# Sums emptied at set later items, and two more passes in 64-row mode, in a fused convolution and two-layer kernel

## The chip, the cores and the metric

The kernel runs on one core of a Trainium2 chip. The metric is device time of one execution in microseconds (us), the median of several runs. The engines are named as in the profile: PE (TensorE, the matmuls), PEld (its weight loads), DVE (VectorE), ACT (ScalarE), POOL (GpSimd) and SP (the queue that issues the DMAs).

## What is computed

A dynamic convolution along the sequence is followed by two fully connected blocks. Cut to what matters:

```python
w = softmax(weight_gen, axis=-1)                 # (2, 4096, 8 heads, 7 taps)
out = einsum('bshk,bskhg->bshg', w, unfolded_x)  # 7 taps back in time, 24 channels a head
x = out.reshape(8192, 192)
h = x @ w_in                                     # 192 -> 2048
g = where(h >= 1, h, where(h <= -1, 0, (h + 1)**2 / 4))
x = g @ w_out                                    # 2048 -> 192: layer 1 ends here
h = x @ w_in2
g = h - tanh(h)
y = g @ w_out2                                   # layer 2
```

Everything is fp32. The kernel keeps that accuracy by splitting each operand into a rounded part (fp32r) and the rest, and multiplying high by high, high by low and low by high.

## The kernel before

The 8192 tokens are cut into 16 blocks of 512. In the code a pass is named by `m` (0 is layer 1, 1 is layer 2) and the block `b`. The 2048 hidden columns of a pass are 16 **items** `f` of 128. An item is: five matmuls into a bank `h` (from `a`, the turned rows of layer 1, or `b`, those of layer 2, and `win`); on ACT and DVE the nonlinearity into `g`; on ACT the high part `gh` (L801); on DVE the low part `gl` (L805; on POOL for some early items); and, some three items later, five matmuls from `gh`, `gl` and `wout` into the two banks of the pass's sum. All 512 items stand in one list, `order`: blocks 0 and 1 of a layer interleaved, and from item 80 on the passes follow one another: layer 1 of block 3 (items 80 to 95), layer 2 of block 2 (96 to 111), layer 1 of block 4 (112 to 127), layer 2 of block 3, and so on to layer 2 of block 15.

A pass runs in one of two ways. In 128-row mode each item's five and five matmuls go one after the other. In **64-row mode** (`paired`, `both`, L693 and L677) two items are taken together and the matmuls are cut into halves of 64 rows, which run two at a time; the third matmul operand of 64 rows then has no idle half, and two items take 19 steps in place of 20. `paired(m, b)` holds from block `MOVED - m` on, so with `MOVED = 4` for layer 1 from block 4 and for layer 2 from block 3.

The convolution of a block (`conv`) runs beside the items of earlier passes, on DVE: softmax of the tap weights, seven tap products (L445), sums (L492). Blocks below `MOVED` are then turned from rows to columns by PE (`transposes`, L530 and L533) and evicted by ACT and DVE (L550 to L562). From block `MOVED` on `move_rows` is used: ACT rounds the rows, DVE turns 32x32 squares of the high and of the low part (L576), and SP writes them to memory and reads them back in the right place (L596 to L607).

When a pass has ended, its sum is emptied: `finish1` (layer 1) makes the next layer's operand, with two ACT evictions, three DVE operations and one or two further ACT copies; `finish2` (layer 2) has one ACT copy (`h1`, L886), a DVE transpose of the first bank (`t0`, L887), a DVE addition (`r`, L888), a DVE transpose of the rest (`t1`, L889) and 24 stores. In 64-row mode these are called from `done`, when the second half of the last items has been multiplied, which is in the fifth and sixth item of the pass that follows.

What an engine does in which order is settled by a planner (`Plan.run`) before the program is written: each task has a key (its due item) and estimated durations, and each engine takes the ready task of the lowest key. The order so found is fixed on the chip; an engine waits at the head of its queue. A dependency that the planner is given, but that no data needs, thus only changes the order. `turn` is such a device: it holds each operation of a convolution back until `gl` of a set item has been planned, one step each `PACE` = 1.3 items, for blocks from `MOVED` on.

Of the kernel before, what the change touches and what calls it, by code (L numbers as in the profile page):

```python
# [20 lines left out]
LAG = 3  # L21
RAW = 4
EARLY = 2
MOVED = 4
REBIAS = 2.0 ** -112
ITEM = 2.275

# [130 lines left out]
def on(engine, dur):  # L158
    return {engine: (dur, 0.0)}
# [3 lines left out]
def tile_dynconv_moe_moe(  # L163
# [18 lines left out]
    NF = FF // P  # L182
    D1 = D - P
# [46 lines left out]
    def x3(s):  # L230

        n, k = divmod(s.n, 2)
        if n not in x3_t:
            x3_t[n] = const.tile([P, 2, N], F32R, tag=f"raw{n}", name=f"x3_{n}")
        return x3_t[n][D1:P, k]
# [14 lines left out]
    plan = Plan()  # L250
# [23 lines left out]
    order = []  # L274
# [10 lines left out]
    marks = {}  # L285
# [81 lines left out]
    xdone = {}  # L367
    a_of, b_of, x3_of = {}, {}, {}
    x3_free = []

    def conv(b, banks, base, gap):
# [7 lines left out]
        count, paced = [0], [0.0]  # L379
# [5 lines left out]
        def turn(k):  # L385

            if b < MOVED:
                return []
            paced[0] += k
            n = int(base + PACE * paced[0])  # L390
            return [marks["gl", it] for it in [order[n]] if n < at[0, b, 0] and ("gl", it) in marks]

        def load_wg(e):
# [38 lines left out]
        t = plan.add(on("DVE", 0.30), key(), lambda e: e.tensor_reduce(MX(), W(), axis=AX.X, op=ALU.max), [lw] + turn(0.5), takes=soft, uses=[wg], own=0.12 if early else 0.0)  # L432
        t = plan.add(on("DVE", 0.30), key(), lambda e: e.tensor_tensor(W(), W(), bc(MX()), op=ALU.subtract), [t] + turn(0.5), uses=[wg] + soft, lock=not early)
        t = plan.add(on("ACT", 0.30), key(), lambda e: e.activation(W(), W(), AF.Exp), [t], uses=[wg])
        t = plan.add(on("DVE", 0.30), key(), lambda e: e.tensor_reduce(SM(), W(), axis=AX.X, op=ALU.add), [t] + turn(0.5), uses=[wg] + soft, own=0.12 if early else 0.0)

        def inverse(e):
# [3 lines left out]
        t = plan.add(on("DVE", 0.47), key(), inverse, [t] + turn(0.5), uses=[wg] + soft, late=0.05, own=0.12 if early else 0.0)  # L441
# [10 lines left out]
        if early:  # L452
# [21 lines left out]
            t = plan.add(on("POOL", 1.55), pk, lambda e: ptap(e, 0, K - 3), [ts, lx, lh], takes=[spare], uses=[wg, xw], late=0.1)  # L474
            t = plan.add(on("POOL", 1.55), pk, lambda e: ptap(e, 1, K - 2), [t], uses=[wg, xw, spare], late=0.1)
# [9 lines left out]
        tasks, sums = [], []  # L485
# [11 lines left out]
        if b == 0:  # L497
            tasks = [tasks[n] for n in (0, 1, 3, 2, 5, 4, 6)]
        for fn, k, kind in tasks:
            last = early and k == mine - 1  # L500
            t = plan.add(
                on("DVE", 0.87), key(), fn, dep + [whole(k), lh] + turn(1.0), takes=([] if kind or k else [mem] + (area2 if b == 0 else [])),
                uses=([] if kind else [wg, xw]) + (more if kind or k or b else area) + ([mem] if kind or k else []),
                late=0.1, own=0.12 if early and b and (k if kind == 0 else last) else 0.0, lock=not early,
            )
# [18 lines left out]
        t = plan.add(on("DVE", 0.97), key(), last_sum, dep + ([pb] if early else []), uses=[mem, xw] + more + ([spare] if early else []), lock=not early)  # L524
# [3 lines left out]
        def transposes(e):  # L528
# [9 lines left out]
            takes=[] if early else area, uses=[mem, xw] + (area if early else []), late=0.4,  # L538
        )
        X = lambda k: xt_t[xt.n][:, k]  # L540
# [19 lines left out]
        h0 = plan.add(on("ACT", 0.48), last, hi0, [tr], takes=[xt], uses=area)  # L560
        h1 = plan.add(on("ACT", 0.76), last, hi1, [h0], uses=area + [xt])
        l0 = plan.add(on("DVE", 0.60), last, lambda e: e.tensor_tensor(X(1), p0, X(0).bitcast(F32), op=ALU.subtract), [h0], uses=area + [xt])  # L562
# [151 lines left out]
    def done(g, t):  # L714

        if g in late2 and late2[g][2] == NF - 1:
            m, b, f, *_, acc, need = late2[g]
            (finish1 if m == 0 else finish2)(b, acc, g + (9.0 if m == 0 else 11.0), t)

    def both(m, b, f, h0, h1, need):  # L720

# [46 lines left out]
    def item(m, b, f, after):  # L768
        i = at[m, b, f]
        h, g, gh, gl = slot("bank", h_banks(m, b)), slot("g"), slot("gh"), slot("gl")  # L770
# [4 lines left out]
        acc = accs[m, b]  # L775
# [10 lines left out]
        elif f % 2 == 0:  # L786
            h1 = slot("bank", h_banks(m, b))
# [6 lines left out]
        if m == 0:  # L794
            t = plan.add(on("ACT", 0.60), i, lambda e: e.activation(G_(), H_(), AF.Relu, bias=0.5, scale=0.5), [first], takes=[g], uses=[h], late=0.1)  # L795
            t = plan.add(on("ACT", 0.537), i, lambda e: e.activation(G_(), G_(), AF.Square), [t], uses=[g])  # L796
            t = plan.add(on("DVE", 0.605), i, lambda e: e.scalar_tensor_tensor(G_(), H_(), 1.0, G_(), op0=ALU.max, op1=ALU.min), [t], uses=[g, h])  # L797
        else:
            t = plan.add(on("ACT", 0.49), i, lambda e: e.activation(G_(), H_(), AF.Tanh), [first], takes=[g], uses=[h])  # L799
            t = plan.add(on("DVE", 0.605), i, lambda e: e.tensor_tensor(G_(), H_(), G_(), op=ALU.subtract), [t], uses=[g, h])  # L800
        thi = plan.add(on("ACT", 0.527), i, lambda e: e.copy(GH(), G_()), [t], takes=[gh], uses=[g])  # L801
# [3 lines left out]
        tlo = plan.add(engines, i, lambda e: e.tensor_tensor(GL(), G_(), GH().bitcast(F32), op=ALU.subtract), [thi], takes=[gl], uses=[g], lock=True)  # L805

        marks["gl", (m, b, f)] = tlo
        w = wout[m][:, f, :]
        a, z = f == 0, f == NF - 1
        need = [wdone.get((1, m, f // 2)), prev2.get((m, b))]  # L810
# [3 lines left out]
        if m == 0 or b < NB - 1:  # L814
# [11 lines left out]
            t = plan.add(on("PE", 0.681), i + LAG + 0.5, mm2a, [thi] + need, takes=acc if a else [], uses=[gh] + ([] if a else acc), late=0.0)  # L826
            t = plan.add(on("PE", 0.454), i + LAG + 0.5, mm2b, [t, tlo], uses=[gl] + acc, late=0.35)
        else:
# [10 lines left out]
            t = plan.add(on("PE", 1.14), i + LAG + 0.5, mm2, [thi, tlo] + need, takes=acc if a else [], uses=[gh, gl] + ([] if a else acc), late=0.35)  # L839
# [2 lines left out]
            (finish1 if m == 0 else finish2 if b < NB - 1 else finish_last)(b, acc, i + LAG + 0.6, t)  # L842
        return first

    def finish1(b, acc, key, t):
        s, tm = slot("xt"), slot("val")
        b_of[b] = s
        X, M = lambda k: xt_t[s.n][:, k], lambda: vals[tm.n][0:D1]
        p0, p1 = lambda: ps[acc[0].n], lambda: ps[acc[1].n]

        def hi(e):
            xt_tile(s, f"b_{b}")
            e.copy(X(0), p0())

        h0 = plan.add(on("ACT", 0.60), key, hi, [t], takes=[s], uses=acc)
        h1 = plan.add(on("ACT", 0.60), key, lambda e: e.copy(M(), p1()[D1:P]), [t], takes=[tm], uses=acc)
        l0 = plan.add(on("DVE", 0.60), key, lambda e: e.tensor_tensor(X(1), p0(), X(0).bitcast(F32), op=ALU.subtract), [h0], uses=acc + [s])
        r = plan.add(on("DVE", 0.60), key, lambda e: e.tensor_tensor(M(), p1()[0:D1], M(), op=ALU.add), [h1], uses=acc + [tm])
        rh = plan.add(on("ACT", 0.525), key, lambda e: e.copy(X(2)[0:D1], M()), [r], uses=[s, tm])
        rl = plan.add(on("DVE", 0.60), key, lambda e: e.tensor_tensor(X(2)[D1:P], M(), X(2)[0:D1].bitcast(F32), op=ALU.subtract), [rh], uses=[s, tm])  # L860
        marks["fin1", b] = r
        xdone[1, b] = [h0, l0, rh, rl]
        if paired(1, b):
            s3 = x3_of[1, b] = slot("x3")
            xdone[1, b].append(plan.add(on("ACT", 0.525), key, lambda e: e.copy(x3(s3), M()), [r] + x3_free, takes=[s3], uses=[tm]))

    def out_raws():

        return (0, 1)

    def finish2(b, acc, key, t):

        s, tm = slot("raw", out_raws), slot("val")
        R = lambda: raws[s.n].rearrange("p a b -> p (a b)").bitcast(F32)
        M = lambda: vals[tm.n][0:D1]
        p0, p1 = lambda: ps[acc[0].n], lambda: ps[acc[1].n]

        def store(e, c):
            r = R()[c * 32:(c + 1) * 32, 0:N] if c < P // 32 else R()[c * 32 - P:c * 32 - P + 32, N:]
            r = r.rearrange("p (u v c) -> p u v c", u=T, c=32)  # L880
            for n in range(T):

                o = out_sq[:, :, b * T + n, c * 32:(c + 1) * 32]
                e.dma_start(o, r[:, :, n] if b >= MOVED else r[:, n])

        h1 = plan.add(on("ACT", 0.60), key, lambda e: e.copy(M(), p1()[D1:P]), [t], takes=[tm], uses=acc)  # L886
        t0 = plan.add(on("DVE", 0.60), key, lambda e: e.transpose(R()[:, 0:N], p0()), [t], takes=[s], uses=acc)  # L887
        r = plan.add(on("DVE", 0.60), key, lambda e: e.tensor_tensor(M(), p1()[0:D1], M(), op=ALU.add), [h1], uses=acc + [tm])  # L888
        t1 = plan.add(on("DVE", 0.60), key, lambda e: e.transpose(R()[0:D1, N:], M()), [r, t0], uses=[s, tm])  # L889
        for c in range(D // 32):  # L890
            plan.add(on("DMA", 2.6), key, lambda e, c=c: store(e, c), [t0 if c < P // 32 else t1], uses=[s], late=3.0)

# [29 lines left out]
    for n, (m, b) in enumerate(streams):  # L922
# [5 lines left out]
        for f in range(NF):  # L928
# [9 lines left out]
            if (m, b, f) == (1, NB - 2, NF - 1):  # L938
                close(at[m, b, f] + 1)

    tasks = plan.run()
    with tc.manual_schedule():
        for t in tasks:
# [4 lines left out]
UNTIL = 3.5  # L948
SKEW = 12
SKEW2 = 12  # L950
BASE3, BASE = 40.0, 40.0
PACE = 1.3
LEAD = (4.0, 6.0)
CONV1 = (0.0, 0.35)
# [30 lines left out]
```

## Time and profile before

| | |
|---|---|
| median of 3 runs | 1182.35 us (1181.68 to 1183.67) |
| the profiled execution | 1182.38 us, span of its trace 1180.6 us |
| busy: PE / DVE / ACT / POOL | 97% / 84% / 72% / 8% of the span |
| granted TensorE clock | 0.995 over the span |

The profiled execution has 1.78 us outside the span of its trace. Busy time of PE counts matmuls that run side by side once. The tables of stages name stretches of the span; the border of a pass is the start of its first matmul from `win`.

### The profile page before, as it was taken

How to read it: one execution, taken by the hardware profiler on the slowest of the kernel's cores; microseconds unless marked ns; L12 is line 12 of the kernel's file. 1: busy time of each engine (PE TensorE's matmuls, PEld its weight loads, DVE VectorE, ACT ScalarE, POOL GpSimd, SP SyncE). 2: the span in 40 equal slices, each digit the busy share in tenths (PEclk: the TensorE clock that was granted, in tenths of full speed). 3: DMA queues.
4: the chain of work that ended last, by engine and by line, in shares of the span. 5: the costliest groups of instructions: out<-in, count | busy, mean ns of one | idle time of the engine just before them, and what ended most of it. 6: DMA issues, size and time to landing. Idle time of an engine off the chain costs nothing.

```text
span 1180.6 us, 23472 instructions
## 1 busy us (share of the span) xinstructions
PE 1144.8 (97%) x8648; PEld 1027.2 (87%) x8648; DVE 995.9 (84%) x1523; ACT 849.1 (72%) x1511; POOL 94.0 (8%) x81
## 2 busy tenths in 40 slices
PE   3899999999999999999999999999999999999998
PEld 2677888888998998889989888999989999999987
DVE  8998998887988879898888989889888888976665
ACT  4989996675867767677676867767686676767653
POOL 4744451000000000000000000000000000000000
PEclk9899999999999999999999999999999999999999
DMA  6522130211130301203021130301213020110000
GB/s 206 161 71 79 54 121 8 52 50 48 19 92 13 89 11 32 79 15 96 9 53 51 19 92 15 96 4 33 76 19 92 12 62 1 27 47 15 1 10 19
DMA packets 93034, 60.50 MB, mean 51 GB/s; under 512 B 56060, under 2 KB 81274, under 8 KB 92920
## 3 DMA queue, kind: packets, MB, share of 16 engines
q1 hardware_dynamic: 92732, 58.62, 18.1%
q8 instruction: 68, 1.11, 0.4%
q10 hardware_dynamic: 188, 0.39, 0.1%
q14 instruction: 46, 0.38, 0.1%
HBM read 43.24 MB, written 15.73 MB: 50 GB/s over the span
## 4 chain that ended last, share of the span: by engine, by line
PE 87%; ACT 6%; DVE 4%; issue 1%; POOL 1%; DMA 1%; DVEq 0%; ACTq 0%
PE ps L677 36%; PE ps L693 31%; PE ps L781 10%; PE ps L823 2%; PE ps L824 2%; PE ps L817 2%; PE ps L818 2%; PE ps L819 2%; ACT g L795 1%; ACT g L796 1%; ACT gh L801 1%; PE ps L834 1%; DVE gl L805 1%; DVE raw L887 1%; ACT val L886 1%
## 5 line engine op out<-in xcount | busy, mean ns | idle before, releaser
L677 PE MATMUL ps<-gh,wout 64*128 64x512 f32 x2304 | 731.9, 387 | 0.0
L677 PE MATMUL ps<-gl,wout 64*128 64x512 f32 x1536 | 597.8, 389 | 3.2 <-DVE gl L805 3.1
L677 PEld LDWEIGHTS ps<-gh,wout 64*128 64x128 f32 x2304 | 421.8, 184 | 26.4 <-ACT gh L801 0.3
L693 PE MATMUL ps<-a,win 64*128 64x512 f32 x1632 | 408.7, 389 | 0.0
L693 PE MATMUL ps<-b,win 64*128 64x512 f32 x1632 | 403.1, 387 | 0.0
L801 ACT CAST gh<-g 128x512 fp32r<-128x512 f32 x512 | 314.3, 617 | 105.1 <-PE ps L677 40.6
L805 DVE TENSOR_TENSOR gl<-g,gh 128x512 fp32r<-128x512 f32 x476 | 327.5, 692 | 41.4 <-ACT gh L801 26.2
L693 PEld LDWEIGHTS ps<-a,win 64*128 64x128 f32 x1632 | 298.1, 184 | 14.4 <-issue 0.4
L693 PEld LDWEIGHTS ps<-b,win 64*128 64x128 f32 x1632 | 300.2, 184 | 5.6
L677 PEld LDWEIGHTS ps<-gl,wout 64*128 64x128 f32 x1536 | 282.7, 184 | 19.7 <-DVE gl L805 12.1
L799 ACT ACTIVATE g<-ps 128x512 f32<-128x512 f32 x256 | 152.8, 598 | 132.6 <-PE ps L693 115.0
L800 DVE TENSOR_TENSOR g<-ps,g 128x512 f32<-128x512 f32 x256 | 174.0, 686 | 67.7 <-ACT g L799 66.5
L797 DVE SCALAR_TENSOR_TENSOR g<-ps,g 128x512 f32<-128x512 f32 x256 | 174.6, 685 | 47.5 <-ACT g L796 44.8
L795 ACT ACTIVATE g<-ps 128x512 f32<-128x512 f32 x256 | 151.5, 592 | 53.5 <-PE ps L693 38.7
L796 ACT ACTIVATE g<-g 128x512 f32<-128x512 f32 x256 | 161.9, 632 | 6.5
L781 PE MATMUL ps<-a,win 128*128 128x512 f32 x320 | 88.0, 411 | 6.2 <-POOL win L351 3.1
L781 PE MATMUL ps<-b,win 128*128 128x512 f32 x320 | 83.3, 391 | 0.0
L781 PEld LDWEIGHTS ps<-a,win 128*128 128x128 f32 x320 | 62.7, 198 | 23.4 <-POOL win L351 4.3
L445 DVE TENSOR_TENSOR prod<-xw,wg 128x768 f32<-128x768 f32 x84 | 80.9, 963 | 0.0
L693 PE MATMUL ps<-x,win 64*128 64x512 f32 x192 | 74.3, 387 | 0.0
L781 PEld LDWEIGHTS ps<-b,win 128*128 128x128 f32 x320 | 59.1, 188 | 12.0 <-issue 0.4
L492 DVE TENSOR_TENSOR acc<-acc,prod 128x768 f32<-128x768 f32 x70 | 67.4, 963 | 0.0
(89 smaller groups left out, 890.4 us busy)
## 6 DMA issues: line engine op xcount, KB each, us to landing
xw<-in_x_dram SPq DMA_DIRECT2D x14, 960.0 KB, 7.0
spot<-xw SPq DMA_DIRECT2D x96, 96.0 KB, 2.0
raw<-in_moe_w_out_dram SPq DMA_DIRECT2D x16, 384.0 KB, 3.1
a<-spot SPq DMA_DIRECT2D x24, 256.0 KB, 3.3
out_dram<-raw SPq DMA_DIRECT2D x360, 16.0 KB, 1.5
raw<-in_moe_w_in_dram SPq DMA_DIRECT2D x16, 256.0 KB, 3.4
raw<-in_moe_w_in_dram SPq DMA_DIRECT2D x32, 128.0 KB, 3.4
a<-spot SPq DMA_DIRECT2D x24, 128.0 KB, 3.3
```

The source lines that it names most:

```text
L445: e.tensor_tensor(dst.rearrange("p j (h g) -> p j h g", h=H), xws[xw.n][:, k:k + T, :].rearrange("p j (h g) -> p j h g", h=H), w[:, :, :, ...
L492: e.tensor_tensor(prods[k % 2] if early and k == mine - 1 else acc_sb, acc_sb, prods[k % 2], op=ALU.add)
L677: return e.matmul(to(), w[rs, c:c + P], (GL() if low else GH())[rs], start=f == 0 and lane == 0 and n == 0, stop=f == NF - 1 and lane == 1 ...
L693: return e.matmul(ps[h.n], win[m][rs, k, fs], x, start=lane == 0 and n == 0, stop=lane == 1 and n == len(ops) - 1)
L781: e.matmul(ps[h.n], w[:, k, fs], xt[:, c], start=n == 0, stop=n == 4)
L795: t = plan.add(on("ACT", 0.60), i, lambda e: e.activation(G_(), H_(), AF.Relu, bias=0.5, scale=0.5), [first], takes=[g], uses=[h], late=0.1)
L796: t = plan.add(on("ACT", 0.537), i, lambda e: e.activation(G_(), G_(), AF.Square), [t], uses=[g])
L797: t = plan.add(on("DVE", 0.605), i, lambda e: e.scalar_tensor_tensor(G_(), H_(), 1.0, G_(), op0=ALU.max, op1=ALU.min), [t], uses=[g, h])
L799: t = plan.add(on("ACT", 0.49), i, lambda e: e.activation(G_(), H_(), AF.Tanh), [first], takes=[g], uses=[h])
L800: t = plan.add(on("DVE", 0.605), i, lambda e: e.tensor_tensor(G_(), H_(), G_(), op=ALU.subtract), [t], uses=[g, h])
L801: thi = plan.add(on("ACT", 0.527), i, lambda e: e.copy(GH(), G_()), [t], takes=[gh], uses=[g])
L805: tlo = plan.add(engines, i, lambda e: e.tensor_tensor(GL(), G_(), GH().bitcast(F32), op=ALU.subtract), [thi], takes=[gl], uses=[g], lock= ...
```

## The change

It has four parts. `MOVED` goes from 4 to 3: layer 1 of block 3 and layer 2 of block 2 run in 64-row mode, block 3's rows go through `move_rows`, and its convolution is paced. Its base is 44 items ahead of its pass, not 40. `turn` no longer names the fourth to seventh item of a pass. And `hold` gives the planner a dependency for each step of emptying a sum in 64-row mode: with `g` the last item of the ended pass, `h1` comes after `gh` of item g+4, `r` after `gl` of g+5, `t0` after `gl` of g+6, `t1` after `gl` of g+7, and likewise in `finish1`. With it the copy of `x3` (a second copy of 64 rows that 64-row mode needs) is made from the rounded part.

```diff
-MOVED = 4
+MOVED = 3
         def turn(k):
             if b < MOVED:
                 return []
-            paced[0] += k
-            n = int(base + PACE * paced[0])
+            paced[0] += k * PACE
+            while int(base + paced[0]) % NF in (3, 4, 5, 6):
+                paced[0] += 1.0
+            n = int(base + paced[0])
             return [marks["gl", it] for it in [order[n]] if n < at[0, b, 0] and ("gl", it) in marks]
     def done(g, t):
-            (finish1 if m == 0 else finish2)(b, acc, g + (9.0 if m == 0 else 11.0), t)
+            (finish1 if m == 0 else finish2)(b, acc, g + (9.0 if m == 0 else 11.0), t, g)
         marks["gl", (m, b, f)] = tlo
+        marks["gh", (m, b, f)] = thi
+    held = []
+    def hold(g, tasks):
+        if g is not None:
+            held.extend((t, kind, g + n) for t, kind, n in tasks)
-    def finish1(b, acc, key, t):
+    def finish1(b, acc, key, t, g=None):
+        hold(g, [(h1, "gh", 4), (r, "gl", 5), (h0, "gh", 5), (l0, "gl", 6), (rh, "gh", 6), (rl, "gl", 7)])
-            xdone[1, b].append(plan.add(on("ACT", 0.525), key, lambda e: e.copy(x3(s3), M()), [r] + x3_free, takes=[s3], uses=[tm]))
+            xdone[1, b].append(plan.add(on("ACT", 0.525), key, lambda e: e.copy(x3(s3), X(2)[0:D1]), [rh] + x3_free, takes=[s3], uses=[s]))
-    def finish2(b, acc, key, t):
+    def finish2(b, acc, key, t, g=None):
+        hold(g, [(h1, "gh", 4), (r, "gl", 5), (t0, "gl", 6), (t1, "gl", 7)])
+    for t, kind, n in held:
+        t.deps.append(marks[kind, order[n]])
     tasks = plan.run()
-BASE3, BASE = 40.0, 40.0
+BASE3, BASE = 44.0, 40.0
```

## Rows read from the trace of the kernel before

**Rows 1.** The page, part 4: the chain that ended last, by engine.
```profile
PE 87%; ACT 6%; DVE 4%; issue 1%; POOL 1%; DMA 1%; DVEq 0%; ACTq 0%
```
**Rows 2.** Table of stages: stretch, length, then busy us (instructions) of PE, PEld, DVE, ACT, POOL.
```profile
217.75:290.38 72.63, 72.63 (x322) 59.90 (x320) 60.56 (x94) 50.02 (x87) 0.00 (x0) 1.00 0.16 45
360.61:396.14 35.53, 35.25 (x306) 31.65 (x305) 31.82 (x47) 27.75 (x48) 0.00 (x0) 1.00 0.09 16
396.14:430.81 34.67, 34.67 (x306) 34.05 (x305) 28.53 (x46) 22.50 (x40) 0.00 (x0) 1.00 0.27 78
1062.81:1097.48 34.67, 34.67 (x306) 33.99 (x305) 22.88 (x35) 27.57 (x48) 0.00 (x0) 1.00 0.08 13
217.75:1062.81 845.06, 841.86 (x6999) 768.30 (x6999) 720.66 (x1096) 601.50 (x1041) 0.00 (x0) 1.00 0.17 44
```
**Rows 3.** The chain of waits, 366 to 450: start, length, engine, tile, line.
```profile
371.45 0.59 ACT val L886
372.06 0.72 DVE raw L887
```
**Rows 4.** Timeline of PE, 371.9 to 374.3: start, length, operation, [idle before, releaser].
```profile
372.74 0.39 PE L693 MATMUL ps<-a,win 64*128 64x512 f32 x1
...
373.41 0.50 PE L677 MATMUL ps<-gl,wout 64*128 64x512 f32 x1 [0.28 <-DVE gl L805]
```
**Rows 5.** Timeline of DVE, 1072.9 to 1077.5.
```profile
1073.63 0.68 DVE L805 TENSOR_TENSOR gl<-g,gh 128x512 fp32r<-128x512 f32 x1
1074.23 0.71 DVE L887 STREAM_TRANSPOSE raw<-ps 128x512 f32<-128x512 f32 x1
```
**Rows 6.** Timeline of PE, 198.3 to 200.
```profile
198.64 0.39 PE L824 MATMUL ps<-gl,wout 128*128 128x512 f32 x1
...
199.50 0.70 PE L781 MATMUL ps<-b,win 128*128 128x512 f32 x2
```
**Rows 7.** Table of stages, columns as in Rows 2: the stages ahead of item 80.
```profile
20.29:104.00 83.71, 75.92 (x299) 58.52 (x300) 79.24 (x123) 75.59 (x153) 45.92 (x38) 0.96 0.37 116
104.00:188.50 84.50, 84.31 (x375) 69.40 (x374) 81.97 (x126) 78.29 (x157) 40.19 (x33) 1.00 0.24 77
188.50:217.75 29.25, 29.25 (x133) 24.13 (x132) 23.51 (x41) 17.44 (x31) 0.00 (x0) 1.00 0.19 48
```
**Rows 8.** Groups by line on DVE, 104 to 125: busy us, mean ns, idle before.
```profile
L438 DVE TENSOR_SCALAR sm<-sm 128x32 f32<-128x32 f32 x1 | 1.2, 1186 | 0.0
L445 DVE TENSOR_TENSOR prod<-xw,wg 128x768 f32<-128x768 f32 x1 | 0.9, 949 | 0.0
```
**Rows 9.** Timeline of all engines, 120.5 to 121.6.
```profile
118.42 2.66 POOL L805 TENSOR_TENSOR gl<-g,gh 128x512 fp32r<-128x512 f32 x1 [0.60 <-POOL gl L805]
...
120.56 0.39 PE L819 MATMUL ps<-gh,wout 128*128 128x512 f32 x1
...
121.14 0.50 PE L823 MATMUL ps<-gl,wout 128*128 128x512 f32 x1 [0.19 <-POOL gl L805]
```
**Rows 10.** Timeline of all engines, 181.5 to 183.5.
```profile
181.71 0.68 DVE L805 TENSOR_TENSOR gl<-g,gh 128x512 fp32r<-128x512 f32 x1
...
183.22 0.39 PE L823 MATMUL ps<-gl,wout 128*128 128x512 f32 x1
```
**Rows 11.** Groups by line, whole span: DVE's 32x32 squares, POOL's low parts.
```profile
L576 DVE STREAM_TRANSPOSE xw<-prod 128x768 f32<-128x768 f32 x12 | 11.7, 978 | 0.4
L805 POOL TENSOR_TENSOR gl<-g,gh 128x512 fp32r<-128x512 f32 x36 | 51.0, 1424 | 54.4 <-ACT gh L801 39.9 <-DVE val L331 5.0 <-DVE prod L445 3.8
```
**Rows 12.** Timeline of DVE and SP, 401 to 410: the last step of one block's rows.
```profile
402.75 0.97 DVE L576 STREAM_TRANSPOSE xw<-acc 128x768 f32<-128x768 f32 x1
407.88 0.45 SPq L605 DMA_DIRECT2D a<-spot  x1
```
**Rows 13.** The page, part 6: the reads of moved rows: KB each, us to landing.
```profile
a<-spot SPq DMA_DIRECT2D x24, 128.0 KB, 3.3
```
**Rows 14.** Timeline of SP, 190 to 220: the stores of block 0.
```profile
198.21 12.74 SPq L884 DMA_DIRECT2D out_dram<-raw  x24
```

## The prediction

> **What bounds the kernel now.** First the chain that ended last: 87% of the span lies on PE, 6% on ACT and 4% on DVE [rows 1]. So time comes off where PE has fewer steps, or where it stands still in front of another engine; work taken from DVE or ACT is worth nothing unless PE waits for it.
>
> Second the table of stages, cut at the borders of the passes [rows 2]. Items 80 to 463 are 24 passes from 217.75 to 1062.81, 845.06 us. The first two, layer 1 of block 3 and layer 2 of block 2, run in 128-row mode: 72.63 us together, PE busy for all of it, 36.3 each. A pass of layer 2 in 64-row mode takes 34.67 with PE never idle. A pass of layer 1 in 64-row mode takes 35.53, with 0.28 idle. The reader is to see that these differ although they have the same matmuls: 0.86 is lost in each layer 1 pass. The last layer 1 pass (block 15), however, takes 34.67 too (the fourth of [rows 2]). It empties a layer 2 sum like all the others, and the one thing that it lacks is a convolution beside it, as there is no block 16 or 17.
>
> Third the chain of waits and the timelines around one loss. The chain leaves PE for ACT's copy of the ended sum (L886, 371.45), goes on to DVE's transpose of it (L887, 372.06) and only then to the low parts that PE wants [rows 3]. PE's next step, due at 372.97 (0.23 after 372.74), starts at 373.41 [rows 4]. Thus the transpose stands in DVE's queue ahead of two low parts and waits for ACT. In the pass without a convolution it stands behind the first low part, 1074.23 after 1073.63 [rows 5], and PE waits for nothing. This is the place that `hold` works on.
>
> Ahead of item 80 it is different: from 104 to 188.5 PE is busy 84.31 of 84.50, but DVE 81.97 as well [rows 7]; two engines are full there. From 188.5 to 217.75 DVE has 23.51 of 29.25.
>
> **The change part by part.** The sum is made against the profiled execution, 1182.38 us (span 1180.6 and 1.78 around it), which is the median of the runs (1182.35) to 0.03.
>
> *Items 80 to 463.* Afterwards all 24 passes are in 64-row mode. With the sums out of the way each takes 34.67: 24 x 34.67 = 832.1 in place of 845.06 [rows 2], 13.0 less. Of this 72.63 - 2 x 34.67 = 3.3 is the mode of the two passes, the other 9.7 the loss in the 11 layer 1 passes beside a convolution. The change of mode itself only moves from item 112 to item 80; as it is part of the passes replaced here, 0.2 is given back for it, an estimate (the loss of 0.86 bounds it above; that pass shows no more). So 12.8.
>
> Why I take the whole 9.7: `hold` puts the copy behind `gh` of g+4, the addition behind `gl` of g+5, the two transposes behind `gl` of g+6 and g+7, one step per item, and `turn` keeps convolution operations off just these items (f = 3 to 6). DVE then has three operations of about 0.7 [rows 5] spread over a stretch from which it loses about three convolution operations of 0.95 [rows 8]. That is less work than it has there now, and the pass without a convolution does it without loss, in an even tighter order. Nobody waits for these steps: the banks that they free are next written a whole pass later. What is queued behind the held copy on ACT are the activations of g+5, and the copy takes ACT some 0.6 [rows 3]. The convolution still has its 1.3 items between steps; it only ends later (below). Bounds: nothing is gained (0) and all of it (9.7). I take all, as the fourth row of [rows 2] is the same pass with the same sum.
>
> *Block 3's turn by PE goes.* Between the last matmul ahead of it (198.64) and the next (199.50) lie the six transposes: 0.86 - 0.23 = 0.6 us on a busy PE [rows 6]. Certain, since the instructions are gone. Its evictions go from ACT and DVE, unseen by PE.
>
> *Block 3's rows by DVE, ACT and SP.* New are an addition, a subtraction and two square transposes, 0.95 to 0.98 each [rows 8, 11], where one last addition was; so 2 to 2.9 more until the subtraction, with evictions saved after that. They are paced up to item 71. The block's eight writes and five reads (from the code) go into SP's queue next to the 24 stores of block 0, which hold it for 12.74 us from 198.21 [rows 14]. From the last square transpose (402.75) to the last read issued (407.88), with 3.3 to land, a block needs 8.5 us [rows 12, 13]. The transpose held to `gl` of item 71 stands at about 201 to 203: the item starts nine steps of 72.63 / 32 = 2.27 ahead of 217.75, at 197.3, and its five matmuls, two ACT and two DVE operations take 5 x 0.23 + 2 x 0.6 + 2 x 0.7 = 3.7 [rows 3 to 5], or up to 6 where they queue. So the rows lie there by 210 to 212, some 2 later if a group of four stores cuts in. Layer 1 of block 3 starts at 217.75: hidden, with 3 us to spare; without that cover it is one delay, by as much as they are late. The extra `x3` copy for block 2 is one ACT copy with 30 items to spare: nothing.
>
> *Block 3's convolution is held back.* This is the part with an open price. Now it runs whenever DVE is free: from 104 to 125 DVE did its reciprocal step (1.2), two products and a sum (0.9 each, the product's row stands for all three) [rows 8], 4 us. Afterwards its first step waits for `gl` of item 39, so these come later, into a stretch where DVE is full. Bounds: against me, 4 us and the 2.9 above arrive and nothing comes back; of those 6.9, the idle 2.5 of DVE between 104 and 188.5 [rows 7] and the 0.8 by which a low part is ready before PE takes it (ended 182.39, used 183.22 [rows 10]) hide 3.3: PE loses 3.6. For me, item work moves up as the convolution moves out, so that all comes back, and a wait of PE goes: at 121.14 it started 0.35 late because a low part on POOL had taken 2.66 [rows 9], against 1.42 on the mean [rows 11], while DVE ran block 3's sums beside it. That gives -0.4. I take +0.6: nearer to the second, since DVE's queue in that stretch was never empty, so most of the freed time is used at once.
>
> On that POOL row the Trainium skill, "GPSIMD Engine Reference", 1. Specifications, says that GpSimd shares its SBUF interfaces with VectorE and is held up by VectorE instructions with two SBUF inputs. By that rule all of block 3's products and sums that leave the stretch of POOL's low parts are a gain, and this term would be -0.4; the row agrees with the rule, but not on how full DVE is later.
>
> *Sum:* -12.8 - 0.6 + 0.6 = -12.8; 1182.4 - 12.8 = **1169.6 us**, a span of 1167.8.
>
> **The rivals.**
> *Full DVE ahead of item 80.* The open price at its upper bound: 1182.4 - 13.4 + 3.6 = 1172.6. For it speaks 81.97 of 84.50; against it that in the stretch before 188.5 DVE already lags and PE is busy for all but 0.2 us [rows 7].
>
> *The losses stay, in part.* If the cause is not the place of the transpose but DVE's load beside a convolution, the 9.7 comes back at another item. Half of it gives 1174.5, all of it 1179.3; that is also the time if the planner's order does not follow the new dependencies. For it: the pass without loss lacks the convolution, not the order. Against it: the chain names the transpose [rows 3].
>
> *Slower: moved rows come late in every block.* Since `turn` jumps four items twice, a convolution that ended 16 items ahead of its pass now ends about 9 ahead, in the eighth item of the layer 2 pass. In the pass 396.14 to 430.81 [rows 2] that item's matmuls end with the fourth pair, at 396.14 + 34.67 / 2 = 413.5, its low part comes some 2.6 later, and from the start of the transpose it is 8.5 us until the rows lie there [rows 12, 13]: 424.6, with 6.2 us to spare. Only if a move takes over 6.2 us longer does each of the 13 layer 1 passes start late, and from 6.2 + 13.4 / 13 = 7.2 on the kernel is slower than before; at 9 us longer it is 1182.4 - 13.4 + 13 x 2.8 = 1205. The trace shows nothing that would take them so long.
> The Trainium skill, "VectorE: DVE Perf Modes", The three transpose paths, speaks for this: it sends a 128x128 transpose to TensorE and warns that a plain DMA whose strides do the turning is 19 times slower than the transposing one. The trace disagrees here: these DMAs land in 3.3 us [rows 13]; the turn within a square of 32x32 is made by DVE before them.
>
> **How the numbers follow.** Forecast 0.60 (by itself 1168 to 1171.5); full DVE 0.18 (to 1173); losses stay 0.15 (1173 to 1179.5); slower 0.05; 0.02 for no change. The low end is the sum with -0.4 in place of +0.6, and some 2 less if the freed DVE time also shortens the start, where PE is idle for 7.8 of 83.7 us and DVE busy for 79.2 [rows 7]: 1166.5. The high end takes in the full DVE and half of the losses: 1175. Slower by over 0.2% (2.4 us, about what a measurement of this kernel can tell from no change) is 0.05; between -2.4 and +2.4 lie only the worst of the losses, 0.03; faster 0.92.
>
> **What would show it.** Each layer 1 pass from item 80 on is 34.67 long; the waits of PE for low parts are gone there; L887 no longer waits for L886; none of PE's transposes is left for block 3; DVE is full until some us after 188.5 with PE unbroken; the border of item 80 lies at 217.75 or up to 1 us on either side. If PE still waits about 0.4 us or more in layer 1 passes, at whatever item, the second rival holds; if item 80 starts 2 us or more later than now, the first; if PE stands still at the start of layer 1 passes, the third. The prediction would be wrong above all if the order of the planner puts another step ahead of a low part that PE is waiting for.

## The result and the profile after

| | before | after |
|---|---|---|
| median of the runs on one chip | 1182.07 us (1181.68 to 1183.67, 4 runs) | 1169.25 us (1168.95 to 1169.47, 4 runs) |
| the profiled execution | 1182.38 us, span 1180.6 | 1169.47 us, span 1167.7 |
| start of item 80 | 217.75 us | 223.25 us |
| items 80 to 463 | 845.06 us | 827.03 us |
| span behind item 463 | 117.8 us | 117.4 us |

The ratio is 0.9889, with an interval of 0.9874 to 0.9905: faster by 1.1%. The forecast was 1169.6. The last three rows of the table add up to the same total by other parts than those of the forecast: item 80 starts 5.5 us later (forecast: 0), and items 80 to 463 take 18.0 less (forecast: 12.8).

Lines of the kernel after: matmuls L679 (second layer, 64 rows), L695 (first layer, 64 rows), L783 and L820 to L827 (the same two in 128-row mode); the low part L807, the high part L803, `g` L797 to L802; convolution products L447, sums L494, squares L578; emptying a layer 2 sum L897 (copy), L899 (addition), L898 and L900 (transposes); weights L326 and L331.

The table of stages of after, columns as in [rows 2]. First items 80 to 463, to be held against [rows 2]:

```profile
223.25:292.31 69.06, 69.06 (x600) 66.47 (x601) 58.69 (x91) 50.00 (x85) 0.00 (x0) 1.00 0.20 59
361.21:395.67 34.46, 34.46 (x307) 33.44 (x305) 29.44 (x45) 27.95 (x48) 0.00 (x0) 1.00 0.08 13
1050.28:1084.74 34.46, 34.46 (x308) 33.44 (x306) 22.66 (x35) 27.63 (x48) 0.00 (x0) 1.00 0.08 13
223.25:1050.28 827.03, 827.03 (x7288) 801.95 (x7289) 717.23 (x1096) 611.76 (x1041) 0.00 (x0) 1.00 0.17 46
```

PE is busy for all of the 827.03, and the list of its waits is empty there. A layer 1 pass beside a convolution (the second row) is now as long as the one without (the third). But both are 34.46, not the 34.67 that such a pass took before. Then the stages ahead of item 80, which answer to [rows 7]:

```profile
20.29:104.00 83.71, 74.23 (x300) 56.62 (x301) 76.12 (x111) 75.38 (x153) 61.13 (x49) 0.98 0.39 123
104.00:188.50 84.50, 81.49 (x352) 65.00 (x350) 75.64 (x116) 74.56 (x148) 34.19 (x28) 1.00 0.22 68
188.50:223.25 34.75, 34.39 (x148) 27.20 (x148) 31.67 (x52) 22.40 (x40) 4.04 (x4) 1.00 0.29 71
```

In the middle row PE has lost 2.8 us of work (84.31 before), and DVE 6.3 (81.97). Over the whole row DVE is not busier; it is busy at the wrong time. Cut finer, the same two engines:

```profile
125.00:144.24 19.24, 19.24 (x87) 15.93 (x85) 15.96 (x26) 17.92 (x36) 6.59 (x6) 1.00 0.15 49
144.24:185.26 41.02, 38.12 (x162) 29.45 (x160) 40.31 (x63) 33.65 (x69) 19.11 (x15) 1.00 0.28 87
```

DVE has 3.3 us to spare in the first stretch and then 0.7 in 41.0, in which PE stands still for 2.9. One of the stops, in five lines picked from the timeline of all engines:

```profile
148.45 0.57 ACT L801 ACTIVATE g<-ps 128x512 f32<-128x512 f32 x1
149.08 0.94 DVE L447 TENSOR_TENSOR prod<-xw,wg 128x768 f32<-128x768 f32 x1
149.95 0.68 DVE L326 SCALAR_TENSOR_TENSOR ps<-ps,raw 128x512 uint32<-128x512 uint32 x1
150.55 0.67 DVE L802 TENSOR_TENSOR g<-ps,g 128x512 f32<-128x512 f32 x1
151.27 0.50 PE L783 MATMUL ps<-b,win 128*128 128x512 f32 x1 [1.21 <-DVE g L802]
```

ACT was done with `g` at 149.02. The subtraction on DVE that frees the bank begins at 150.55, because a product of block 3's convolution and a step of the weights stand ahead of it in DVE's queue; PE waits 1.21 us for that bank. The list of PE's waits from 104 to 223 has six stops, 3.3 us in all, the first at 151.27 and the last at 199.45 (columns: the waiter, its releaser, us in total, times, the longest). Only one of them is for a bank that `g` on DVE frees:

```profile
PE ps L783 <- DVE g L802: 1.2, 1, 1.2
PE ps L820 <- ACT gh L803: 1.1, 1, 1.1
PE ps L826 <- DVE gl L807: 0.4, 2, 0.3
PE ps L821 <- DVE wout L351: 0.4, 1, 0.4
PE ps L783 <- DVE val L331: 0.2, 1, 0.2
```

The place that `hold` works on, which was [rows 3] and [rows 5]; DVE in the layer 1 pass 361.21 to 395.67:

```profile
376.44 0.68 DVE L807 TENSOR_TENSOR gl<-g,gh 128x512 fp32r<-128x512 f32 x1
377.04 0.68 DVE L899 TENSOR_TENSOR val<-ps,val 64x512 f32<-64x512 f32 x1
377.64 0.67 DVE L807 TENSOR_TENSOR gl<-g,gh 128x512 fp32r<-128x512 f32 x1
378.24 0.70 DVE L898 STREAM_TRANSPOSE raw<-ps 128x512 f32<-128x512 f32 x1
```

Each step stands behind a low part, and the copy on ACT (L897) had begun at 372.78 and took 0.58: the transpose waits for nobody.

### The profile page after: what moved, and what is told of

It is laid out like the page before. It is cut to its first block, busy times and chain, and to the rows that moved or that the text cites. A ratio compares the mean times of both kernels' runs of the same rounds, so it can differ in the third digit from the quotient of the medians.

```text
span 1167.7 us, 24235 instructions
## 1 busy us (share of the span) xinstructions
PE 1130.1 (97%) x8930; PEld 1056.4 (90%) x8930; DVE 991.0 (85%) x1513; ACT 860.5 (74%) x1510; POOL 107.1 (9%) x90
## 4 chain that ended last, share of the span: by engine, by line
PE 83%; DVE 1%; issue 0%; DVEq 0%
PE ps L679 41%; PE ps L695 36%; PE ps L783 3%; PE ps L837 1%; PE ps L838 0%; DVE gl L807 0%; PE ps L826 0%; PE ps L827 0%; PE ps L821 0%; PE ps L820 0%; PE ps L822 0%; DVE g L802 0%; DVE raw L913 0%; DVE acc L494 0%; DVE val L331 0%
## 5 line engine op out<-in xcount | busy, mean ns | idle before, releaser
L679 PE MATMUL ps<-gh,wout 64*128 64x512 f32 x2496 | 809.7, 386 | 0.0
L679 PE MATMUL ps<-gl,wout 64*128 64x512 f32 x1664 | 642.3, 386 | 0.0
L679 PEld LDWEIGHTS ps<-gh,wout 64*128 64x128 f32 x2496 | 449.0, 184 | 18.0
L695 PE MATMUL ps<-b,win 64*128 64x512 f32 x1768 | 433.9, 386 | 0.0
L695 PE MATMUL ps<-a,win 64*128 64x512 f32 x1768 | 433.7, 386 | 0.0
L803 ACT CAST gh<-g 128x512 fp32r<-128x512 f32 x512 | 315.1, 617 | 85.6 <-DVE g L802 29.5
L807 DVE TENSOR_TENSOR gl<-g,gh 128x512 fp32r<-128x512 f32 x474 | 327.8, 692 | 27.8 <-ACT gh L803 20.4
L695 PEld LDWEIGHTS ps<-a,win 64*128 64x128 f32 x1768 | 318.9, 184 | 5.1 <-issue 0.4
L695 PEld LDWEIGHTS ps<-b,win 64*128 64x128 f32 x1768 | 319.1, 184 | 4.4
L679 PEld LDWEIGHTS ps<-gl,wout 64*128 64x128 f32 x1664 | 306.2, 184 | 0.3
L802 DVE TENSOR_TENSOR g<-ps,g 128x512 f32<-128x512 f32 x256 | 171.3, 682 | 53.7 <-ACT g L801 51.9
L797 ACT ACTIVATE g<-ps 128x512 f32<-128x512 f32 x256 | 151.8, 593 | 50.5 <-PE ps L695 31.2
L447 DVE TENSOR_TENSOR prod<-xw,wg 128x768 f32<-128x768 f32 x84 | 85.0, 1012 | 0.0
L695 PE MATMUL ps<-x,win 64*128 64x512 f32 x208 | 80.3, 386 | 0.0
L783 PE MATMUL ps<-a,win 128*128 128x512 f32 x240 | 65.9, 407 | 9.4 <-POOL win L351 3.2
L494 DVE TENSOR_TENSOR acc<-acc,prod 128x768 f32<-128x768 f32 x70 | 69.7, 996 | 0.0
L783 PEld LDWEIGHTS ps<-a,win 128*128 128x128 f32 x240 | 46.0, 195 | 23.9 <-POOL win L351 4.3
L783 PE MATMUL ps<-b,win 128*128 128x512 f32 x240 | 62.7, 394 | 1.4 <-DVE g L802 1.2
L807 POOL TENSOR_TENSOR gl<-g,gh 128x512 fp32r<-128x512 f32 x38 | 55.6, 1469 | 48.8 <-ACT gh L803 21.1
```

The costliest lines, as they stand in the source:

```text
L447: e.tensor_tensor(dst.rearrange("p j (h g) -> p j h g", h=H), xws[xw.n][:, k:k + T, :].rearrange("p j (h g) -> p j h g", h=H), w[:, :, :, ...
L494: e.tensor_tensor(prods[k % 2] if early and k == mine - 1 else acc_sb, acc_sb, prods[k % 2], op=ALU.add)
L679: return e.matmul(to(), w[rs, c:c + P], (GL() if low else GH())[rs], start=f == 0 and lane == 0 and n == 0, stop=f == NF - 1 and lane == 1 ...
L695: return e.matmul(ps[h.n], win[m][rs, k, fs], x, start=lane == 0 and n == 0, stop=lane == 1 and n == len(ops) - 1)
L783: e.matmul(ps[h.n], w[:, k, fs], xt[:, c], start=n == 0, stop=n == 4)
```

## Experiments

The kernels below start from the changed one; the kernel before took 1181.6 to 1183.6 us beside them. They ran on four chips: order_only, no_hold, no_jump and one_stop on a first, same_again and the three kernels with a freed or swapped order on a second, the two cut kernels and turned_by_pe on a third, turned_halved_44 on a fourth.

**The change once more.** same_again has the same instructions in the same order as the changed kernel.

> The kernel after the change, every order on every engine the same (ties of the planner are broken by a running number in place of an address, which gives the same plan). Two arrangements of the two halves of PE have been seen, 34.45 and 34.67 us for a pass. If the arrangement belongs to the program: 1169.3 us in every run, passes of 34.45. If it is settled by chance in each execution: some runs about 24 x 0.22 = 5.2 us longer, near 1174.5.

Measured: 1174.91 us (6 runs), ratio 0.9927 (0.9913 to 0.9942). One execution, the profiled one, took 1169.25 and has passes of 34.45; the other five took 1174.21 to 1176.15. The first four of the changed kernel had all been near 1169.2. So one program has two times, 5 to 7 us apart. 24 passes of 34.67 in place of 34.45 would make 5.3 of that; none of the five longer executions has a trace, so that these are their passes is an inference. PE's timeline shows what differs between traces of either length, at the same place of after (34.45), order_only (34.67) and order_only_swapped (34.67), both below. Here `wout` goes through the upper 64 rows and `win` through the lower:

```profile
559.72 0.39 PE L679 MATMUL ps<-gl,wout 64*128 64x512 f32 x1
559.78 0.39 PE L695 MATMUL ps<-b,win 64*128 64x512 f32 x1
559.95 0.39 PE L679 MATMUL ps<-gh,wout 64*128 64x512 f32 x1
```
```profile
559.75 0.39 PE L698 MATMUL ps<-b,win 64*128 64x512 f32 x1
559.82 0.39 PE L682 MATMUL ps<-gl,wout 64*128 64x512 f32 x1
559.97 0.39 PE L698 MATMUL ps<-b,win 64*128 64x512 f32 x1
```
```profile
559.72 0.39 PE L682 MATMUL ps<-gl,wout 64*128 64x512 f32 x1
559.80 0.39 PE L698 MATMUL ps<-b,win 64*128 64x512 f32 x1
559.95 0.39 PE L682 MATMUL ps<-gh,wout 64*128 64x512 f32 x1
```

In the first the lower half follows the upper by 0.057 us in all pairs of items but the first, and a pair takes 4.307 (19 x 0.2267). In the second the lower half is ahead in all but the first few pairs, mostly by 0.05 to 0.08, and in the third the upper, by 0.08; in both a pair takes 4.333.

**The order alone.** `MOVED` and the base as before; `hold` and the jump kept.

```diff
-MOVED = 3
+MOVED = 4
-BASE3, BASE = 44.0, 40.0
+BASE3, BASE = 40.0, 40.0
```

> Only the emptying of the sums and the jumps of turn are kept; MOVED is 4 and block 3's base 40 as in the kernel before. Theory A (a stop of PE puts the two halves of 64-row mode into an arrangement in which two items take 4.33 us, and without any stop after the entry they stay at 4.31): item 80 comes at 217.75 as before, the two passes after it take 72.6, and the 22 passes in 64-row mode 34.45 each, so 1182.1 - 14.3 = 1167.8 us, less than with the whole change. Theory B (the shorter passes come from block 3's new way): 34.67 each, 1172.4 us.

Measured: 1172.76 us (1172.40 to 1172.88, 4 runs), ratio 0.9916 (0.9902 to 0.9931). Item 80 starts at 217.91, as before.

```profile
217.91:254.18 36.27, 36.27 (x161) 30.04 (x160) 29.32 (x44) 27.25 (x49) 0.00 (x0) 1.00 0.07 12
290.54:325.31 34.77, 34.77 (x295) 31.80 (x296) 28.02 (x43) 26.78 (x46) 0.00 (x0) 1.00 0.08 13
359.98:394.66 34.68, 34.68 (x307) 34.06 (x306) 29.42 (x45) 27.82 (x48) 0.00 (x0) 1.00 0.08 14
```

A layer 1 pass in 64-row mode no longer loses anything (third row), and the entry into the mode costs 0.1 (second). PE's list of waits is empty from item 80 on and the passes are still 34.67, so theory A falls. The gain of the order by itself is 1182.4 - 1172.8 = 9.6 us (9.9 against the 1182.63 of the kernel before beside it); the forecast had 9.7 for it.

**No dependencies on the emptying.**

```diff
     for t, kind, n in held:
-        t.deps.append(marks[kind, order[n]])
+        pass
```

> The planner is not given the dependencies of hold; the rest of the change stays. If the place of the transpose is the cause, as the prediction took it: 0.6 to 0.9 us lost again in each layer 1 pass beside a convolution, the passes in between at 34.67, so about 12 x 0.86 + 24 x 0.22 = 15 us more, 1184 us. If the convolution's operations at items 4 to 7 of a pass are the cause: no loss, 1169.3 us.

Measured: 1182.37 us (1181.54 to 1183.02, 10 runs), ratio 0.9998 (0.9988 to 1.0007). A pass of layer 1 beside a convolution takes 35.30, one of layer 2 34.67. The 12 losses of 0.63 make 7.6, and with 1174.9 for the change that gives 1182.5: the whole gain of the change goes. PE's list of waits from 222.7 to 1062 has the old culprit back, once in each of the 12 passes (L810 is the low part there; the columns are the waiter, its releaser, us in total, times and the longest):

```profile
PE ps L682 <- DVE gl L810: 3.4, 12, 0.3
```

On DVE the transpose (L901) stands ahead of two low parts again and waits for the copy on ACT (L900):

```profile
374.16 0.72 DVE L901 STREAM_TRANSPOSE raw<-ps 128x512 f32<-128x512 f32 x1 [0.55 <-ACT val L900]
374.80 1.25 DVE L810 TENSOR_TENSOR gl<-g,gh 128x512 fp32r<-128x512 f32 x2
```

**The jump for block 3 alone.**

```diff
-            while int(base + paced[0]) % NF in (3, 4, 5, 6):
+            while b == 3 and int(base + paced[0]) % NF in (3, 4, 5, 6):
```

> turn jumps items 4 to 7 of a pass only for block 3; hold stays. If hold is enough: passes of 34.45 and 1169.3 us. If the convolution has to be kept away as well: PE waits for low parts in the layer 1 passes, by 0.3 to 0.9 us each, and the passes in between take 34.67: 1175 to 1184 us.

Measured: 1175.57 us (1175.21 to 1176.88, 4 runs), ratio 0.9943 (0.9928 to 0.9958). Most layer 1 passes take 34.68 to 34.79, one 35.03: some 1.0 us over 12 passes, 0.08 each. PE's list of waits is empty there, so what the 0.08 consists of isn't shown. Without `hold` a pass loses 0.63, without the jump 0.08; the median time by itself lies among the changed kernel's longer executions (1174.2 to 1176.2) and shows no loss.

**One stop.** To see whether a stop of PE decides the arrangement of the halves, one low part of block 3's layer 2 (its item 4) is written six times.

> The subtraction that makes the low part of the fifth item of layer 2 of block 3 is written six times in a row (same result), which stops PE once for about 3.0 us less some slack; every order is as after the change. Theory A: this pass is 1 to 2.5 us longer, and all 21 passes behind it take 34.67 in place of 34.45, 4.6 us more: 1175 to 1176.5 us. Theory B (only the stop itself costs): 1170.3 to 1171.8 us, later passes at 34.45.

Measured: 1178.28 us (1176.64 to 1180.04, 6 runs), ratio 0.9963 (0.9951 to 0.9975). One pass is 4.0 longer; all others but the first, which has the entry (34.76), are 34.65 to 34.67, those ahead of the stop too. The long arrangement was there ahead of the stop, so it needs none; whether a stop could end the short one was not seen.

**Block 3 not held back.** `move_rows` and the base of 44 stay, but `turn` leaves block 3 free. The swapped kernels issue the upper half first in each pair of matmuls.

```diff
-            if b < MOVED:
+            if b < MOVED + 1:
                 return []
```
```diff
-            for lane, ops in ((0, low), (1, high)):
+            for lane, ops in ((1, high), (0, low)):
```

> Block 3's convolution is not held back by turn (all later blocks are), everything else as after the change. If holding it back is what costs the 5.5 us ahead of item 80 (VectorE idle for some 8 us between 104 and 144, and then too full): item 80 at 217 to 219 in place of 223.25, so 1164 to 1165.5 us with passes of 34.45, or 1169 to 1170.5 with passes of 34.67. If it is the added work of block 3's moved rows: item 80 at 221 or later.

> free_conv3 with the same swap of the issue order. Theory C: passes of 34.45 in all 24 passes and item 80 at 217 to 219, so 1164 to 1165.5 us, the best so far. Theory D: 1169 to 1170.5 us, or as free_conv3.

> order_only (1172.8 us, passes of 34.67 from its entry on) with one line more: in each step the matmul of the upper 64 rows is issued ahead of that of the lower 64 rows. Theory C (the step is short when the upper half leads, and the issue order settles who leads): the 22 passes take 34.45, 4.8 us less, 1168.0 us. Theory D (the lead is chance and the issue order has no say, or a lead of either half can be long): 1172.8 us as without it.

Measured, in this order: 1173.36 us (1171.65 to 1176.03, 4 runs), 1172.07 (1171.39 to 1173.65, 4 runs) and 1172.62 (1172.00 to 1172.81, 4 runs); ratios 0.9916, 0.9912 and 0.9913 (each give or take 0.0015). All three profiled executions have passes of 34.67. In the two swapped ones the upper half is ahead, by 0.08: the order of issue changes who is ahead, but not the length. Item 80 starts at 224.19, 220.88 and 217.92. So the pacing of block 3 isn't needed for its delay. The first two have the same plan ahead of item 80, and yet are 3.3 apart. They part first where DVE and POOL begin within 0.03 us of each other (first two lines), and again at a later sum (third line); free_conv3, then free_conv3_swapped:

```profile
148.10 2.08 DVE L450 TENSOR_TENSOR prod<-xw,wg 128x768 f32<-128x768 f32 x1
148.07 1.29 POOL L810 TENSOR_TENSOR gl<-g,gh 128x512 fp32r<-128x512 f32 x1 [0.45 <-ACT gh L806]
151.77 1.93 DVE L586 TENSOR_TENSOR acc<-acc,prod 128x768 f32<-128x768 f32 x1
```
```profile
148.07 0.94 DVE L450 TENSOR_TENSOR prod<-xw,wg 128x768 f32<-128x768 f32 x1
148.07 2.10 POOL L810 TENSOR_TENSOR gl<-g,gh 128x512 fp32r<-128x512 f32 x1 [0.47 <-ACT gh L806]
150.60 0.94 DVE L586 TENSOR_TENSOR acc<-acc,prod 128x768 f32<-128x768 f32 x1
```

One of the two takes longer, DVE by 1.1 or POOL by 0.8; where it is DVE, its whole queue moves. Three such meetings make up the 3.3: DVE took 2.08, 1.93 and (at 171.90) 1.42 us in free_conv3, and 0.94, 0.94 and 0.28 in the other. In free_conv3 POOL had begun first each time, by 0.03, 0.20 and 0.03 us, and kept its 1.3; in the other DVE had begun first or within 1 ns, and kept its time.

**The lower half pushed back.** At the entry into 64-row mode six matmuls of the lower half are cut in two, in order_only and in the whole change, so that the upper half gets ahead.

```diff
+                if n in halve:
+                    for a in (0, N // 2):
+                        q = e.matmul(to()[:, a:a + N // 2], w[rs, c:c + P], (GL() if low else GH())[rs, a:a + N // 2], start=False, stop=False)
+                    return q
-            low = second(0, 0, g0, P_KINDS) + second(0, 1, g0, Q_KINDS)
+            low = second(0, 0, g0, P_KINDS, () if have else (1, 2)) + second(0, 1, g0, Q_KINDS, () if have else (1,))
...
```

> The kernel of order_only with one thing changed: at the entry into 64-row mode (item 112) six matmuls of the lower half, three for each of the two items multiplied there, are each cut into two of 256 columns, so that the lower half falls some 0.05 to 0.1 us behind the upper one. Theory L (which half is ahead decides the length of a pair of items, 4.307 with the upper half ahead, 4.333 without, and it stays so): passes from item 128 on are 34.45 instead of 34.67, the matmuls of the upper half are some 0.06 us ahead, and the time is 1172.7 - 22 x 0.22 = 1167.9. Rival (who is ahead has no say, the arrangement comes from elsewhere): passes 34.67, time 1172.7 (to 1172.9 with the cut).

> The whole change with the same cut of six lower-half matmuls at its entry into 64-row mode (item 80). Theory L: passes 34.45 in every execution, so 1169.3 in each run and no run near 1175; item 80 still at 221 to 224. Rival: as in same_again, most runs 1174 to 1176.

Measured: 1168.68 us (1167.34 to 1169.54, 4 runs), ratio 0.9887 (0.9872 to 0.9902), where order_only had never been under 1172; and 1169.45 (1169.22, 1169.29, 1169.61 and one of 1173.17), ratio 0.9902 (0.9887 to 0.9917). Both profiles have 0.11 between the halves after the entry, then 0.057 and pairs of 4.307 from the third pair on. So theory L came out in both, at 0.1 us for the push. That the push did it is not shown: turned_by_pe, on the same chip and without it, has 34.45 in its profile too, while order_only and same_again ran on other chips.

**Block 3 turned by PE, its passes in 64-row mode.** Block 3's convolution as before (base 40, unpaced, six transposes), and four small copies on ACT that give 64-row mode its second operand.

```diff
-MOVED = 3
+MOVED = 4
+PAIR = 3
-        return b >= MOVED - m and (m, b) != (1, NB - 1)
+        return b >= PAIR - m and (m, b) != (1, NB - 1)
-BASE3, BASE = 44.0, 40.0
+BASE3, BASE = 40.0, 40.0
...
```

> The whole change, but block 3's convolution as before: base 40, not paced, its rows turned by TensorE; its passes still in 64-row mode, for which ACT makes the extra copy (four small copies of 64x256). Theory A (what delays item 80 is the work of moving block 3's rows, and when it is done): item 80 at 217.9, give or take 0.7, as in order_only (217.91), two passes of 34.67 in place of 72.6, time 1172.7 - 3.3 = 1169.4 with passes of 34.67 and 1164 with passes of 34.45. Theory B (the delay has to do with the mode of the next passes or with the new order elsewhere): item 80 at 221 to 224 as in the whole change, time 1173 to 1175.

Measured: 1166.92 us (1164.32 to 1167.85, 4 runs), ratio 0.9876 (0.9859 to 0.9892): the fastest kernel here.

```profile
144.24:185.26 41.02, 41.02 (x183) 33.97 (x182) 39.69 (x63) 37.54 (x80) 21.90 (x20) 1.00 0.30 90
217.98:252.59 34.61, 34.61 (x297) 33.05 (x297) 28.83 (x44) 27.49 (x48) 0.00 (x0) 1.00 0.08 13
252.59:287.04 34.45, 34.45 (x307) 33.43 (x305) 30.68 (x49) 23.16 (x40) 0.00 (x0) 1.00 0.28 83
```

Item 80 is back at 217.98 with PE unbroken from 144 to 185, and the two passes take 34.61 and 34.45 in place of 36.27 and 36.36. The delay of item 80 thus has nothing to do with the mode or with `hold`: it comes from the moved rows of block 3, from its base, or from its pacing on top of them. The three runs without a profile (1166.13 to 1167.85) lie between this and the 1169.6 that 24 passes of 34.67 would give (1164.3 + 24 x 0.22); why, no trace tells.

**The base by itself.** The same with base 44, and the six matmuls cut.

```diff
-BASE3, BASE = 40.0, 40.0
+BASE3, BASE = 44.0, 40.0
```

> turned_by_pe with two things changed: block 3's convolution with base 44 instead of 40 (not paced, as before), and six lower-half matmuls cut in two at the entry into 64-row mode, as in order_only_halved. On item 80: theory A (the added work of the moved rows is what delays it): the border stays at 217.9, give or take 0.7. Theory B (the earlier base is): 221 to 224. On the halves: theory L (the half that is ahead at the entry decides): passes 34.45 and with A 1164.3 in nearly every run, none above 1166; rival: runs spread between 1164 and 1169 as in turned_by_pe (1164.32 to 1167.85). With B and L 1168 to 1170.

Measured: 1173.41 us (1172.67 to 1176.12, 5 runs), ratio 0.9931 (0.9918 to 0.9945). Item 80 starts at 220.93, 3.0 later than in turned_by_pe: the base alone, without pacing and moved rows, costs 3.0 us in this execution, the fastest of the five. The stage, PE's waits from 104 to 221, and DVE and PE at the longer of them:

```profile
104.00:188.50 84.50, 82.91 (x359) 65.70 (x358) 79.99 (x119) 77.45 (x155) 45.31 (x35) 1.00 0.25 77
```
```profile
PE ps L803 <- DVE g L819: 1.4, 2, 1.1
```
```profile
112.28 1.33 DVE L451 TENSOR_TENSOR prod<-xw,wg 128x768 f32<-128x768 f32 x1
113.54 0.68 DVE L819 SCALAR_TENSOR_TENSOR g<-ps,g 128x512 f32<-128x512 f32 x1
114.27 0.50 PE L803 MATMUL ps<-a,win 128*128 128x512 f32 x1 [1.08 <-DVE g L819]
```

It is the same sort of stop as the one shown of after: a bank that `g` on DVE frees late, behind a product of block 3. But the two lie at 114.27 and 132.69, where after has none; after's lie from 151 to 199. All five profiled executions of base 40 have item 80 at 217.75 to 217.98, all nine of base 44 at 220.88 to 224.19. The passes are 34.67 here in spite of the cut: the halves stood 0.08 apart from the second pair on, upper ahead, and from about 385 us on the lower was ahead, by 0.05 to 0.06, with no change in the length. So the theory that the half which is ahead decides falls in that form; what goes with 4.307 in every profile is the lower half 0.057 behind. Going by their times, seven of the eight executions of the two kernels with the cut before this one were short, and none of the five here, which ran on another chip: chance, the chip and the cut are not told apart.

## Why the prediction was right, and where it was wrong

The total was right (1169.6, measured 1169.25), but two terms were off by about 5 us each and cancelled.

*The order: right.* The 9.7 was measured alone as 9.6 (order_only). The cause named, transposes ahead of low parts, is confirmed by no_hold, which keeps the jump and gives back 7.6, the old order and the old wait. The jump on top of it is worth 1.0 us by the passes of no_jump's one trace. The rival that the losses stay is out.

*The mode of two passes: right.* 3.3 less 0.2; turned_by_pe has the two passes with an entry of 0.16 (34.61 - 34.45).

*The transposes: right.* After has none for block 3 (the last two begin at 100.48 and 100.59, for block 2).

*Block 3's convolution is held back: wrong.* The step took +0.6, with 3.6 as its worst. Item 80 starts 5.5 later although 0.6 of transposes are gone, so it measured +6.1 in this profile. I priced how much work arrives in a full stretch and how much idle time of DVE takes it. But that the base moves was only told, never priced: with it each step of block 3's convolution has a key four items lower, and the planner puts it ahead of item work that PE is waiting for. That is near what the prediction named last as its weak point, another step ahead of one that PE wants. Turned_halved_44 shows 3.0 us for the base without pacing, by stops ahead of 144; in after PE is never idle from 104 to 144, block 3's products and sums run later than before (138 to 199 us, before 113 to 177), and the stops lie among them. So for the changed kernel itself the share of the base, of the pacing and of the moved rows in the 6.1 stays open, as does that of chance, since one plan alone varied by 3.3; neither moved rows nor pacing with base 40 was run. The rival "full DVE ahead of item 80" was right on the place and too low on the price (2 us or more later was its mark).
The forecast's -0.4, by the rule of the Trainium skill ("GPSIMD Engine Reference", 1. Specifications: interfaces shared by GpSimd and VectorE), has the effect right, but block 3's work did not leave the stretch in which POOL works beside it, and DVE can be the one held up: rows of two executions show 0.8 to 1.1 us for one meeting, on either engine. In after four of block 3's products and sums between 142 and 171 us took 1.49 to 2.05 us beside POOL, 3.2 over their 0.95 in all; before, four took 1.03 to 1.47, 1.1 over.

*24 passes of 34.67: wrong in the other direction.* 34.67 was read from the trace of before as the least that a pass can take. After has 34.45, because PE's halves stood 0.057 apart in that execution: 5.2 less (18.0 - 12.8). With this luck gone the forecast's own steps, with 6.1 in place of 0.6, give 1175.1, and that is what five of the ten executions of the changed kernel took (1174.2 to 1176.2).

*Moved rows late: out.* Block 3's last read is issued at 213.01, 10.2 ahead of item 80, and PE is unbroken from there to item 463.

## What to carry to other kernels

When a change shifts the due time of work on an engine that is full, price the shift by itself: look up whose operation the work will now stand ahead of, and who waits for that one; the volume of work says little. An order that keeps low-urgency steps behind the operations that PE waits for was worth 9.6 us here, and one block's convolution with its due time four items earlier cost 3.0. And if the total of a forecast comes out right, add up its parts from the profile and run the program again before believing them.

## What the runs showed of the hardware

Two streams of 64-row matmuls settle in positions relative to each other. At 0.057 us (upper half ahead) a pair of items takes 4.307, and the position lasted from the second or third pair to the end in all five traces that have it. At 0.08 (upper ahead), or with the lower level or up to 0.09 ahead, a pair takes 4.333, 0.6% more, 5 us of this kernel; among these positions a trace can change (turned_halved_44, near 385 us). Which one an execution gets isn't fixed by the program (same_again) or by the order of issue, and the long one needs no stop of PE; whether a push at the entry or the chip shifts the odds is open. Of a DVE and a POOL operation with two inputs in SBUF that met in free_conv3 and its swapped twin, the one that began first kept its time, where the trace tells the two apart (four of six meetings), and the other took longer, DVE by 1.0 to 1.1 us, POOL by 0.1 to 0.8; a lead of 0.03 us was enough. Three such meetings drew two executions of one plan 3.3 us apart by item 80.
